# Retention attention and a Gelu MLP on one core: batches in pairs, units of 128 tokens, attention output made transposed in column tiles

## The chip, the core and the metric

The kernel runs on one core of one Trainium2 chip. The metric is device microseconds of that core for one execution; the median of several runs counts. TensorE (PE) multiplies matrices into PSUM; VectorE (DVE) and ScalarE (ACT) move and scale what lies in PSUM; GpSimd (POOL) issues the loads that convert float32 to bfloat16, and SyncE (SP) issues the other transfers.

## What is computed

A retention layer (attention without softmax, with a decay per head) and then a two-layer MLP with an exact Gelu:

```python
batch, n_heads, seq, head_dim = (8, 8, 576, 64)
scores = (1/sqrt(64)) * q @ k^T                       # per batch and head
gamma  = 1 - 2 ** (-5 - h)
D      = where(i >= j, gamma ** (i - j), 0)
x      = ((scores * D) @ v)  -> [8 * 576, 512]        # heads side by side
out    = gelu(x @ w_in) @ w_out                       # 512 -> 2048 -> 512, float32
```

The decay is separable: gamma^(i-j) = gamma^i * gamma^-j. So the sum over all earlier chunks of 128 tokens can be carried as a 64x64 state per head (sum of k^T v with v scaled), and within a chunk only a triangular mask is needed.

## The kernel before

Everything is written out by hand, in an order that a small planner at the end of the kernel chooses while the program is built; `manual_schedule` keeps that order on every engine. The planner holds one clock, `now`, for TensorE, with a fixed cost for each step, and times at which data should be ready (`at`, `x_at`, `land_chunk`, `land_in`, `land_out`).

Attention goes batch after batch in chunks of 128 tokens; a batch of 576 tokens has four full chunks and one of 64, so there are 40 chunks. For chunk i:
- `load_chunk`: three GpSimd loads (q, k, v); for chunk 0 three SyncE loads in float32.
- `turn` (step T): q and k transposed so that head_dim lies on partitions, on TensorE for the first 9 chunks (L213, copied out in L215 or L217), by a SyncE DMA transpose later (L207).
- `scores` and `masked` (step R, or RR for two chunks): eight matmuls with 64 rows of weights each (L226). Even and odd heads lie on partitions 0-63 and 64-127, so these are *row tiles*: two matmuls use one half of the array each. VectorE multiplies by the mask (L235), two products per chunk.
- `scaled_v` (step V): v times gamma^-j / 8 (L242).
- `inner` (step S): masked scores times v, eight matmuls of 64 columns (L260) with tokens on the output's partitions, and the state, four matmuls of 128 columns (L266) that compute two heads at once with two unused cross blocks; ScalarE copies the state out (L270).
- `cross`: q times the state of the chunks before, eight row-tiled matmuls of 64 columns (L280), added into the same PSUM banks.
- `evacuate`: VectorE scales by gamma^i (L288) into `x`, tokens on partitions. The MLP needs x transposed: `turn_x` on TensorE (step X, L302, copied in L303) for the first 9 chunks, a SyncE DMA transpose (L294) later.

The MLP goes over 9 blocks of 512 tokens. `mlp1_step`: four matmuls per 128 hidden units (L314), then Gelu on ScalarE (L318). `mlp2_step`: 16 matmuls per 128 tokens (L343), copied by ScalarE (L349) and stored by SyncE (L350); the last 128 tokens in three column pieces (L331 to L335). Blocks 0 and 1 are cut into pieces, so that they can start before all their tokens are there. In steady blocks the planner puts attention steps between MLP steps; a step RR stands in the second product of a block.

PSUM's eight banks are split: five (`a` to `e`) for transposes, scores, MLP; two for `o_ps`, one for `u_ps`. In the opening POOL builds an identity, two masks and three zeroed tiles before its first load, then loads chunks 1 to 3, the eight pieces of w_in, chunk 4, and w_out mixed with chunks 5 and 6. TensorE runs `warm` matmuls (L470) on zeros while it waits.

Of the kernel before, what the change touches and what calls it, by code (L numbers as in the profile page):

```python
# [13 lines left out]
ALU = mybir.AluOpType  # L14


@with_exitstack
def kernel(
# [13 lines left out]

# [8 lines left out]

# [4 lines left out]
    TOK_BLK = 512  # L46
    N_BLK = n_tok // TOK_BLK
    NCH = -(-S // C)
    chunks = [(b, ci, ci * C, min(C, S - ci * C)) for b in range(B) for ci in range(NCH)]
    N_CH = len(chunks)  # L50
    N_PE_TR = 9
    N_FIRST = 4
    N_LD = 7
    LEAD = 52
    PAIR_FROM = 2
    PAIR_LEAD = 70
    LATE_LEAD = 48
    log_gamma = [math.log(1.0 - 2.0 ** (-5.0 - h)) for h in range(H)]

    const_pool = ctx.enter_context(tc.tile_pool(name="const", bufs=1))  # L60
    ld_pool = ctx.enter_context(tc.tile_pool(name="ld", bufs=N_LD))
    tr_pool = ctx.enter_context(tc.tile_pool(name="tr", bufs=9))
    ret_pool = ctx.enter_context(tc.tile_pool(name="ret", bufs=2))
    v_pool = ctx.enter_context(tc.tile_pool(name="v", bufs=5))
    x_pool = ctx.enter_context(tc.tile_pool(name="x", bufs=4))
    u_pool = ctx.enter_context(tc.tile_pool(name="u", bufs=4))
    g_pool = ctx.enter_context(tc.tile_pool(name="g", bufs=2))
    o_pool = ctx.enter_context(tc.tile_pool(name="o", bufs=4))

    PS = bass.MemoryType.PSUM  # L70

    ps = ctx.enter_context(tc.tile_pool(name="ps", bufs=1, space=PS))

    xT = const_pool.tile([128, N_DM, n_tok], BF16, name="xT")


    zeros = const_pool.tile([128, 512], BF16, name="zeros")
    nc.vector.memset(zeros, 0.0)

    clock = [0.0]  # L80
    first = []
    for nm, src in (("q32", q), ("k32", k), ("v32", v)):
        t = const_pool.tile([128, H, D], FP32, name=nm)
        nc.sync.dma_start(t, src[0, :, 0:C, :].rearrange("h s d -> s h d"))
        first.append(t)
    ident = const_pool.tile([128, 128], BF16, name="ident")
    make_identity(nc, ident)

    lg_row = const_pool.tile([128, H, 1], FP32, name="lg_row")
    for h in range(H):  # L90
        nc.vector.memset(lg_row[:, h], log_gamma[h])
    ln_scale = const_pool.tile([128, 1], FP32, name="ln_scale")
    nc.vector.memset(ln_scale, math.log(scale))
    msk = const_pool.tile([128, 1, 128], FP32, name="msk")
    nc.vector.memset(msk, 1.0)

    pos = const_pool.tile([128, 1, NCH], FP32, name="pos")
    nc.gpsimd.iota(pos[:, 0, :], pattern=[[C, NCH]], base=0, channel_multiplier=1,
                   allow_small_or_imprecise_dtypes=True)

    nc.gpsimd.affine_select(
        out=msk[:, 0, :], in_=msk[:, 0, :], compare_op=ALU.is_ge, fill=0.0, base=0,
        pattern=[[1, 128]], channel_multiplier=-1,
    )

    arg = const_pool.tile([128, H, NCH], FP32, name="arg")
    nc.vector.tensor_tensor(arg, lg_row.to_broadcast([128, H, NCH]), pos.to_broadcast([128, H, NCH]), op=ALU.mult)
    dv = const_pool.tile([128, H, NCH], FP32, name="dv")
    nc.scalar.activation(dv, arg, AF.Exp, scale=-1.0, bias=ln_scale)
    dq = const_pool.tile([128, H, NCH], FP32, name="dq")  # L110
    nc.scalar.activation(dq, arg, AF.Exp)

    warm_act = const_pool.tile([128, 1], FP32, name="warm_act")
    nc.scalar.activation(warm_act, ln_scale, AF.Gelu)


    ret_short = [const_pool.tile([128, HP, 128], BF16, name=f"ret_short{e}") for e in range(2)]
    vh_short = const_pool.tile([128, H, D], BF16, name="vh_short")
    for t in ret_short + [vh_short]:
        nc.gpsimd.memset(t, 0.0)  # L120


    loaded = {}
    land_chunk, land_in, land_out = {}, [], []
    dma_clock = [2.0]

    def load_chunk(i, now=0.0):
        b, ci, c0, cs = chunks[i]
        qk = ld_pool.tile([128, 2, H, D], BF16, tag="qk", name="qk_ld")
        if i == 0:  # L130
            v_ld = first[2]
            nc.vector.tensor_copy(qk[:, 0], first[0])
            nc.vector.tensor_copy(qk[:, 1], first[1])
        else:
            v_ld = ld_pool.tile([128, H, D], BF16, tag="v", name="v_ld")
            for dst, src in ((qk[:, 0], q), (qk[:, 1], k), (v_ld, v)):
                nc.gpsimd.dma_start(dst[:cs], src[b, :, c0:c0 + cs, :].rearrange("h s d -> s h d"))  # L137
        loaded[i] = (qk, v_ld)
        dma_clock[0] = max(dma_clock[0], now) + 3.0 * cs / C
        v_at = 6.5 if i == 0 else dma_clock[0] + (1.2 if i < N_FIRST else 1.6)  # L140
        land_chunk[i] = (v_at - 1.9, v_at - 0.9, v_at)

    W_IN_COLS = 256
    w_in_sb, w_out_sb = [], []

    def load_w_in():
        j = len(w_in_sb)
        t = const_pool.tile([128, N_DM, W_IN_COLS], BF16, name=f"w_in{j}")
        nc.gpsimd.dma_start(
            t, moe_w_in[:, j * W_IN_COLS:(j + 1) * W_IN_COLS].rearrange("(c p) f -> p c f", p=128)  # L150
        )
        w_in_sb.append(t)
        dma_clock[0] += 1.38
        land_in.append(dma_clock[0] + (1.9 if j else 1.3))

    def load_w_out():
        j = len(w_out_sb)
        t = const_pool.tile([128, 2, d_model], BF16, name=f"w_out{j}")
        nc.gpsimd.dma_start(
            t, moe_w_out[j * 256:(j + 1) * 256, :].rearrange("(c p) f -> p c f", p=128)  # L160
        )
        w_out_sb.append(t)
        dma_clock[0] += 1.38
        land_out.append(dma_clock[0] + 1.3)

    for i in range(4):
        load_chunk(i)
    for _ in range(d_ff // W_IN_COLS):
        load_w_in()
    load_chunk(4)  # L170
    for j in range(N_DF // 2):
        load_w_out()
        if j in (3, 6):
            load_chunk(5 + (j == 6))
    


    st = {i: {} for i in range(N_CH)}
    u_ps = [None]
    mlp_begun = [False]  # L180

    free_at = dict.fromkeys("abcde", 0.0)
    held = set()
    last_tag = [None]

    def first_free(n=1):
        return sorted((x for x in free_at if x not in held), key=lambda x: free_at[x])[:n]

    def bank(until, shape, dtype, name):

        tag = last_tag[0] = first_free()[0]
        free_at[tag] = clock[0] + until
        return ps.tile(shape, dtype, tag=tag, name=name)

    def tr_ps(shape, name):

        return bank(1.3, shape, BF16, name)

    def turn(i, parts=(0, 1)):

        cs = chunks[i][3]
        qk = loaded[i][0]
        if "qkT" not in st[i]:
            st[i]["qkT"] = tr_pool.tile([128, 2, HP, 128], BF16, tag="qkT", name="qkT")
        qkT = st[i]["qkT"]
        if i >= N_PE_TR:
            nc.sync.dma_start(qkT.rearrange("p j hp s -> p (j hp) s")[:, :, :cs],  # L207
                              qk[:cs].rearrange("p j h d -> p (j h d)"), transpose=True)
            return
        for j in parts:  # L210
            ps = tr_ps([128, HP, 128], "qk_ps")
            for hp in range(HP):
                nc.tensor.transpose(ps[:, hp, :cs], qk[:cs, j, 2 * hp:2 * hp + 2, :], ident[:cs, :cs])  # L213
            if i >= N_FIRST:
                nc.vector.tensor_copy(qkT[:, j, :, :cs], ps[:, :, :cs])  # L215
            else:
                nc.scalar.copy(qkT[:, j, :, :cs], ps[:, :, :cs])  # L217

    def scores(i, banks):
        cs = chunks[i][3]  # L220
        qkT = st[i]["qkT"]
        sc = [ps.tile([128, HP, 128], FP32, tag=banks[e], name=f"sc{e}") for e in range(2)]
        for hp in range(HP):
            for e in range(2):
                sl = slice(64 * e, 64 * e + 64)
                nc.tensor.matmul(sc[e][:cs, hp, :cs], lhsT=qkT[sl, 1, hp, :cs], rhs=qkT[sl, 0, hp, :cs],  # L226
                                 start=True, stop=True)
        return sc

    def masked(i, sc):  # L230
        b, ci, c0, cs = chunks[i]
        st[i]["ret"] = []
        for e in range(2):
            r = ret_short[e] if cs < C else ret_pool.tile([128, HP, 128], BF16, tag=f"ret{e}", name=f"ret{e}")
            nc.vector.tensor_tensor(r[:cs, :, :cs], sc[e][:cs, :, :cs],  # L235
                                    msk[:cs, :, :cs].to_broadcast([cs, HP, cs]), op=ALU.mult)
            st[i]["ret"].append(r)

    def scaled_v(i):
        b, ci, c0, cs = chunks[i]  # L240
        vh = vh_short if cs < C else v_pool.tile([128, H, D], BF16, tag="vh", name="vh")
        nc.vector.tensor_tensor(vh[:cs], loaded[i][1][:cs],  # L242
                                dv[:cs, :, ci:ci + 1].to_broadcast([cs, H, D]), op=ALU.mult)
        st[i]["vh"] = vh

    def by_parity(i):

        lo = HP * st[i]["half"]
# [358 lines left out]
```

## Time and profile before

| what | value |
|---|---|
| median of the runs (311.76 to 313.3) | 312.15 us |
| span of the profiled execution | 444.2 us |
| mean granted TensorE clock in it | 0.658 |
| VectorE, ScalarE, GpSimd busy | 101.9, 143.3, 112.4 us |
| packets of GpSimd's loads (60% of 16 engines' span) | 17.97 MB |
| packets of SyncE's transfers (22.5%) | 21.05 MB |
| x transposes by DMA (L294): issues, us to landing | 31, 3.5 |
| q and k transposes by DMA (L207) | 31, 5.0 |
| output stores (L350), 256 KB each | 35, 2.4 |

Each run is timed without the profiler; the profile is one more execution, and this one took longer than the timed ones, at a lower clock. "PEclk" is the clock that TensorE was granted, in tenths of full speed. A line of the timeline gives start, duration, engine, source line, output<-input, and in brackets the idle time before it and what ended that. Matmuls are pipelined, so their durations overlap; the distance between starts is the pace.

### The profile page before, as it was taken

How to read it: one execution, taken by the hardware profiler on the slowest of the kernel's cores; microseconds unless marked ns; L12 is line 12 of the kernel's file. 1: busy time of each engine (PE TensorE's matmuls, PEld its weight loads, DVE VectorE, ACT ScalarE, POOL GpSimd, SP SyncE). 2: the span in 40 equal slices, each digit the busy share in tenths (PEclk: the TensorE clock that was granted, in tenths of full speed). 3: DMA queues.
4: the chain of work that ended last, by engine and by line, in shares of the span. 5: the costliest groups of instructions: out<-in, count | busy, mean ns of one | idle time of the engine just before them, and what ended most of it. 6: DMA issues, size and time to landing. Idle time of an engine off the chain costs nothing.

```text
span 444.2 us, 6130 instructions
## 1 busy us (share of the span) xinstructions
PE 436.6 (98%) x2522; PEld 204.9 (46%) x2522; DVE 101.9 (23%) x189; ACT 143.3 (32%) x279; POOL 112.4 (25%) x144
## 2 busy tenths in 40 slices
PE   7999999999999999999999999999999999999997
PEld 3676358855534444344433443344434333333334
DVE  4601345345332240034402500063102100000000
ACT  5664025523244213421343124311442134114411
POOL 9878524426242316004620440000000000000000
PEclk8666666666666666666666666666666666666666
DMA  9999979959999989519990991042101200010011
GB/s 136 179 189 178 127 107 144 90 62 158 159 154 72 110 105 155 60 35 167 127 161 1 121 176 47 0 84 72 41 0 49 66 25 0 24 47 26 0 46 49
DMA packets 168636, 39.40 MB, mean 89 GB/s; under 512 B 157600, under 2 KB 164128, under 8 KB 168608
## 3 DMA queue, kind: packets, MB, share of 16 engines
q0 software_dynamic: 115792, 17.97, 59.8%
q1 hardware_dynamic: 52816, 21.05, 22.5%
q8 instruction: 19, 0.31, 0.3%
q14 instruction: 9, 0.07, 0.1%
HBM read 36.70 MB, written 9.44 MB: 104 GB/s over the span
## 4 chain that ended last, share of the span: by engine, by line
PE 95%; DVE 2%; DMA 1%; POOL 1%; issue 1%; ACT 0%; DVEq 0%
PE hT L314 42%; PE oT L343 41%; PE o_ps L260 3%; PE u_ps L266 2%; PE o_ps L280 1%; PE oT L331 1%; DMA qk_ld<-in_k_dram 1%; PE qk_ps L213 1%; PE x_ps L302 0%; DVE x L288 0%; DVE vh L242 0%; DVE qkT L215 0%; POOL qk_ld L137 0%; DVE ret_966 L235 0%; DVE ret_425 L235 0%
## 5 line engine op out<-in xcount | busy, mean ns | idle before, releaser
L137 POOL DMA_DIRECT2D qk_ld<-in_q_dram x39 | 33.5, 859 | 143.7 <-PE u_ps L266 107.4
L349 ACT COPY o_sb<-oT 128x512 f32<-128x512 f32 x35 | 20.5, 585 | 138.4 <-PE oT L343 132.7
L137 POOL DMA_DIRECT2D v_ld<-in_v_dram x39 | 34.0, 872 | 1.4 <-DMA w_in_153<-in_moe_w_in_dram 0.7
L137 POOL DMA_DIRECT2D qk_ld<-in_k_dram x39 | 33.6, 861 | 0.9 <-DMA w_in_151<-in_moe_w_in_dram 0.5
L270 ACT CAST u_sb<-u_ps 128x512 bf16<-128x512 f32 x32 | 18.7, 585 | 43.9 <-PE u_ps L266 43.3
L288 DVE TENSOR_TENSOR x<-o_ps,dq 128x512 bf16<-128x512 f32 (+1 forms) x40 | 26.4, 681 | 24.5 <-PE o_ps L280 14.5
L314 PE MATMUL hT<-xT,w_in_149 128*128 128x512 bf16 (+3 forms) x96 | 25.8, 429 | 0.5 <-DMA w_in_149<-in_moe_w_in_dram 0.5
L314 PE MATMUL hT<-xT,w_in_151 128*128 128x512 bf16 (+3 forms) x96 | 26.2, 431 | 0.0
L314 PE MATMUL hT<-xT,w_in_157 128*128 128x512 bf16 (+3 forms) x96 | 26.2, 432 | 0.0
L314 PE MATMUL hT<-xT,w_in_163 128*128 128x512 bf16 (+3 forms) x96 | 26.0, 432 | 0.0
L314 PE MATMUL hT<-xT,w_in_155 128*128 128x512 bf16 (+3 forms) x96 | 26.0, 428 | 0.0
L314 PE MATMUL hT<-xT,w_in_153 128*128 128x512 bf16 (+3 forms) x96 | 25.5, 423 | 0.3 <-DVE qkT L215 0.3
L314 PE MATMUL hT<-xT,w_in_159 128*128 128x512 bf16 (+3 forms) x96 | 25.5, 427 | 0.0
L314 PE MATMUL hT<-xT,w_in_161 128*128 128x512 bf16 (+3 forms) x96 | 25.5, 428 | 0.0
L242 DVE TENSOR_TENSOR vh<-v_ld,dv 128x512 bf16<-128x512 bf16 x31 | 20.8, 678 | 0.0
L314 PEld LDWEIGHTS <-w_in_159 128*128 128x128 bf16 x96 | 10.7, 117 | 13.4 <-issue 12.2
L314 PEld LDWEIGHTS <-w_in_163 128*128 128x128 bf16 x96 | 10.9, 121 | 12.8 <-issue 12.0
L314 PEld LDWEIGHTS <-w_in_157 128*128 128x128 bf16 x96 | 11.1, 122 | 12.5 <-issue 11.5
L314 PEld LDWEIGHTS <-w_in_149 128*128 128x128 bf16 x96 | 10.8, 119 | 12.9 <-issue 11.2
L314 PEld LDWEIGHTS <-w_in_161 128*128 128x128 bf16 x96 | 10.9, 120 | 12.4 <-issue 10.9
L314 PEld LDWEIGHTS <-w_in_155 128*128 128x128 bf16 x96 | 10.9, 121 | 12.2 <-issue 11.2
L314 PEld LDWEIGHTS <-w_in_151 128*128 128x128 bf16 x96 | 11.0, 120 | 11.5 <-issue 10.6
(814 smaller groups left out, 730.3 us busy)
## 6 DMA issues: line engine op xcount, KB each, us to landing
out_dram<-o_sb SPq DMA_DIRECT2D x35, 256.0 KB, 2.4
qk_ld<-in_q_dram POOLq DMA_DIRECT2D x31, 128.0 KB, 5.0
qk_ld<-in_k_dram POOLq DMA_DIRECT2D x31, 128.0 KB, 5.3
v_ld<-in_v_dram POOLq DMA_DIRECT2D x31, 128.0 KB, 5.5
qk_ld<-in_q_dram POOLq DMA_DIRECT2D x8, 64.0 KB, 5.5
qk_ld<-in_k_dram POOLq DMA_DIRECT2D x8, 64.0 KB, 6.2
v_ld<-in_v_dram POOLq DMA_DIRECT2D x8, 64.0 KB, 5.9
qkT<-qk_ld SPq DMA_TRANSPOSE x31, 5.0
```

Source lines behind the costliest of these rows:

```text
L137: nc.gpsimd.dma_start(dst[:cs], src[b, :, c0:c0 + cs, :].rearrange("h s d -> s h d"))
L213: nc.tensor.transpose(ps[:, hp, :cs], qk[:cs, j, 2 * hp:2 * hp + 2, :], ident[:cs, :cs])
L242: nc.vector.tensor_tensor(vh[:cs], loaded[i][1][:cs], dv[:cs, :, ci:ci + 1].to_broadcast([cs, H, D]), op=ALU.mult)
L260: nc.tensor.matmul(ov[:, e, hp, :], lhsT=s["ret"][e][:, hp, :], rhs=s["vh"][:, 2 * hp + e, :], start=(hp == 0 and mate is None), stop=(ci ...
L266: nc.tensor.matmul(u_ps[0][:, hp, :], lhsT=loaded[i][0][:cs, 1, 2 * hp:2 * hp + 2, :], rhs=s["vh"][:cs, 2 * hp:2 * hp + 2, :], start=(ci = ...
L270: nc.scalar.copy(u, u_ps[0])
L280: nc.tensor.matmul(ov[:cs, e, hp, :], lhsT=s["qkT"][sl, 0, hp, :cs], rhs=s["u"][sl, hp, 64 * e:64 * e + 64], start=False, stop=(hp == HP - 1),
L288: nc.vector.tensor_tensor(x.rearrange("p hp e d -> p e hp d")[:cs], by_parity(i)[:cs], dq.rearrange("p (hp e) c -> p e hp c", e=2)[:cs, :, ...
L314: nc.tensor.matmul(hT[:, :hi - lo], lhsT=w[:, cc, o:o + 128], rhs=xT[:, cc, tok0 + lo:tok0 + hi], start=(cc == 0), stop=(cc == N_DM - 1))
L331: nc.tensor.matmul(oT[:, :hi - lo], lhsT=g_tiles[t, m][:, ts * 128:(ts + 1) * 128], rhs=w_out_sb[m // 2][:, m % 2, lo:hi], start=(m == 0), ...
L343: nc.tensor.matmul(oT, lhsT=g_tiles[t, m][:, ts * 128:(ts + 1) * 128], rhs=w_out_sb[m // 2][:, m % 2, :], start=(m == 0), stop=(m == N_DF ...
L349: nc.scalar.copy(o_sb, oT)
```

## The change

Batches are taken in pairs. A *unit* has 128 tokens: (pair, chunk, one of the two batches), and the two 64-token ends of a pair make one unit together, with a mask that keeps the batches apart. That gives 36 units, all full, and 512 MLP tokens are always 4 units; xT's columns are in the order of units, and an output tile of a joined end is stored with two transfers.

The matmuls of attention change sides. In `inner`, v is the weight (64 columns) and the masked scores stream (128 columns), so the output has head_dim on partitions: even heads in partitions 0-63, odd ones in 64-127, which are *column tiles*. The state is made in column tiles too, only the blocks that are used, and ScalarE copies two halves into a block-diagonal tile whose other blocks were zeroed once. `cross` is then four matmuls on the whole array. The output is what the MLP takes, so `evacuate` writes xT directly, and the x transposes and `turn_x` are gone. The scale gamma^i now runs along columns (`dqT`).

```diff
+    for bp in range(B // 2):
+        for ci in range(NCI - 1):
+            groups.append([len(units), len(units) + 1])
+            units += [(bp, ci, 0), (bp, ci, 1)]
+        groups.append([len(units)])
+        units.append((bp, NCI - 1, None))
...
-                nc.tensor.matmul(ov[:, e, hp, :], lhsT=s["ret"][e][:, hp, :], rhs=s["vh"][:, 2 * hp + e, :],
-                                 start=(hp == 0 and mate is None), stop=(ci == 0 and hp == HP - 1), skip_group_check=True)
+                nc.tensor.matmul(o[64 * e:64 * e + 64, hp, :], lhsT=vals[:, 2 * hp + e, :], rhs=s["ret"][e][:, hp, :],
+                                 start=(hp == 0), stop=(ci == 0 and hp == HP - 1), skip_group_check=True)
...
-                nc.tensor.matmul(u_ps[0][:, hp, :], lhsT=loaded[i][0][:cs, 1, 2 * hp:2 * hp + 2, :],
-                                 rhs=s["vh"][:cs, 2 * hp:2 * hp + 2, :], start=(ci == 0 and hp == 0),
+                nc.tensor.matmul(u_ps[64 * e:64 * e + 64, j, hp, :], lhsT=loaded[i][0][:, 1, 2 * hp + e, :],
+                                 rhs=s["vh"][:, 2 * hp + e, :], start=(ci == 0 and j == 0 and hp == 0),
...
-            nc.scalar.copy(u, u_ps[0])
+        u = u_sb[ci % 2]
+        for e in range(2):
+            sl = slice(64 * e, 64 * e + 64)
+            nc.scalar.copy(u[sl, j, :, 64 * e:64 * e + 64], u_ps[sl, j])
...
-                nc.tensor.matmul(ov[:cs, e, hp, :], lhsT=s["qkT"][sl, 0, hp, :cs],
-                                 rhs=s["u"][sl, hp, 64 * e:64 * e + 64], start=False, stop=(hp == HP - 1),
+                nc.tensor.matmul(o[:, hp, cols], lhsT=u[:, jj, hp, :], rhs=s["qkT"][:, 0, hp, cols],
+                                 start=False, stop=(hp == HP - 1), skip_group_check=True)
...
-            nc.sync.dma_start(xT[:, :, col:col + cs], x[:cs].rearrange("p hp e d -> p (hp e d)"), transpose=True)
+            nc.vector.tensor_tensor(dst, o, by, op=ALU.mult)
```

In the numbers of the changed kernel, scores are L281, their masks L294, inner L317, the state L329 and its copies L337, cross L359, evacuation L369 and L377, MLP L393, L398 and L430. Two units (`N_RAW`) at the start take the decay in the mask (`near`) and use v unscaled, and ScalarE copies their output.

The opening: POOL has two iotas ahead of its first load. The identity, masks and exponents are derived from an iota by VectorE and ScalarE; the table `dqT` by four exponentials for its second chunk and by GpSimd products with a step factor for the others. v of the first unit is loaded by GpSimd.

```diff
-    for i in range(4):
-        load_chunk(i)
-    for _ in range(d_ff // W_IN_COLS):
-        load_w_in()
-    load_chunk(4)
-    for j in range(N_DF // 2):
-        load_w_out()
-        if j in (3, 6):
-            load_chunk(5 + (j == 6))
+    ORDER = ("q1 k1 v0 v1 q2 k2 q3 k3 wi0 v2 v3 wi1 wi2 wi3 wi4 wi5 wi6 wi7 dq2 q4 k4 v4 wo0 wo1 wo2 dq3 q5 k5 v5 wo3 wo4 "
+             "q6 k6 v6 wo5 wo6 dq4 dq0 q7 k7 v7 wo7 q8 k8 v8")
...
+    near = const.tile([128, 2, HP, 128], FP32, name="near")
+    nc.scalar.activation(near, arg, AF.Exp, bias=ln_scale)
...
+    for hp in range(HP):
+        nc.scalar.activation(dqT[:, hp, C:2 * C], val[:, 0, :], AF.Exp, scale=lgT[:, hp], bias=off[:, hp])
...
+            nc.gpsimd.tensor_tensor(dqT[:, :, i * C:i * C + n], dqT[:, :, o * C:o * C + n],
+                                    by.to_broadcast([128, HP, n]), op=ALU.mult)
```

The planner is new (the "emission model"): it keeps a clock for TensorE, ScalarE, VectorE and GpSimd each (`T`), adds a cost when TensorE goes between full, row-tiled and column-tiled matmuls (`pe`), and takes all eight PSUM banks as one stock with a time at which each is free (`free_at`, `held`). Its steps are A (scores, for one or two units, with inner, state and cross of the units before when they are ready), B (inner), U (state), X (cross and evacuation) and T (a half of a transpose):

```diff
+            elif kind == "A":
+                g, back = a
+                for i in back:
+                    inner(i)
+                    nB += 1
+                    if units[i][1] < NCI - 1:
+                        to_state.append(i)
+                for i in to_state[:]:
+                    to_state.remove(i)
+                    state(i)
+                for i in g:
+                    scores(i)
+                    nA += 1
+                for n, i in enumerate(g):
+                    masked(i)
+                    if n == 0:
+                        for x in back:
+                            cross(x)
+                            evacuate(x)
+                            nX += 1
```

The first 8 units are transposed on TensorE (`either` copies them out on VectorE or ScalarE, whichever is free first), the other 28 by DMA. MLP blocks 0 and 1 are cut into two halves of 256 tokens.

## The prediction

> **What bounds the kernel now.** I read the page's busy rows and clock row first, then the chain of waits, then the timeline of the opening and of one attention step.
>
> ```profile
> span 444.2 us, 6130 instructions
> ...
> PE 436.6 (98%) x2522; PEld 204.9 (46%) x2522; DVE 101.9 (23%) x189; ACT 143.3 (32%) x279; POOL 112.4 (25%) x144
> ...
> PE   7999999999999999999999999999999999999997
> ...
> PEclk8666666666666666666666666666666666666666
> ...
> PE 95%; DVE 2%; DMA 1%; POOL 1%; issue 1%; ACT 0%; DVEq 0%
> ```
>
> TensorE is busy 98% of the span and is 95% of the chain that ended last. But this execution had a granted clock of about 0.65 and took 444.2 us; the timed runs' median is 312.15. So I count TensorE's work in streamed columns and price them at both clocks. Two pieces of the chain give the slow price:
>
> ```profile
> 357.76 20.91 PE hT L314 x64
> 378.67 20.91 PE oT L343 x64
> ```
>
> 64 matmuls of 512 columns in 20.91 us: 1.567 columns per ns at a granted 0.653, so 2.40 at clock 1.00. A burst in the opening agrees:
>
> ```profile
> 12.18 0.28 PE L260 MATMUL o_ps<-vh,ret_288 128*128 128x64 bf16 x4
> ...
> 12.29 0.28 PE L260 MATMUL o_ps<-vh,ret_290 128*128 128x64 bf16 x4
> ...
> 12.40 0.52 PE L266 MATMUL u_ps<-vh,qk_ld 128*128 128x128 bf16 x4
> ```
>
> Eight 64-column matmuls start between 12.18 and 12.40: 27.5 ns each, 2.33 per ns. The reader is to see also that their eight 128-column weight loads hid behind them.
>
> Columns before. MLP: 1152 x 512 = 589,824. Attention: scores 32 x 512 + 8 x 256 = 18,432 (a pair of row tiles starts together in L226, so it counts once); inner 40 x 512 = 20,480; state 32 x 512 = 16,384; cross 32 x 256 = 8,192 (pairs again); q and k transposes 8 x 1024 + 512 = 8,704; x transposes 8 x 512 + 256 = 4,352. That is 76,544, in all 666,368: 425.2 us at 1.567, 277.7 us at 2.40. So the timed runs hold 312.15 - 277.7 = 34.5 us that is not streaming at full clock (or their mean clock lies between 277.7/312.15 = 0.89 and 1). Of it the trace explains 23.2 us:
> - opening: the first MLP matmul starts at 17.52, after some 10,750 columns of attention (4.5 us at 2.40): 13.0;
> - 33 visits to row tiles, two switches each. In the steady part matmuls follow each other every 0.29 or 0.36 us; the row tile after the one at 158.49 came 0.46 later, at 158.95, so a switch costs 0.11: 66 x 0.11 = 7.3;
> - tail: last matmul ends about 441.3, span 444.2: 2.9.
>
> 11.3 us stay open: a clock just under 1, or waits that a slow TensorE hides here (after 24 us the profile's windows show only 0.85 us of idle TensorE).
>
> ```profile
> 3.25 1.01 POOL qk_ld L137
> 4.26 4.11 DMA qk_ld<-in_k_dram
> ...
> 11.38 0.82 POOL L149 DMA_DIRECT2D w_in_149<-in_moe_w_in_dram  x1
> ...
> 17.52 1.40 PE L314 MATMUL hT<-xT,w_in_149 128*128 128x256 bf16 x8 [0.54 <-DMA w_in_149<-in_moe_w_in_dram]
> ```
>
> The opening hangs on POOL's DMA queue: its first load is issued at 3.2 behind masks and memsets, the first weights at 11.38, and the MLP starts when those land.
>
> **The change, step by step.**
>
> *Columns.* 36 full units replace 40 chunks (64-token ends are joined). Scores 36 x 512 = 18,432. Inner has 8 matmuls of 128 columns with 64-wide weights, whose outputs lie in partitions 0-63 and 64-127; if such column tiles overlap in pairs as the row tiles do, 36 x 512 = 18,432. State 32 x 256 = 8,192 on the same condition. Cross becomes 4 full matmuls of 128 columns (8 of 64 for a joined end) on a block-diagonal state: 28 x 512 = 14,336. Transposes 8 x 1024 = 8,192; x transposes none. Total 67,584: 8,960 fewer, -5.7 us at 1.567 and **-3.7 us** at 2.40. No row here shows a column tile. Bounds by the nearest rows: full overlap as in L226; none as in L260 adds 18,432 + 8,192 = 26,624 columns, +11.1 us. I take full overlap, because operands and sizes are nearest to the row tiles.
>
> The trace first: six loads of 64-wide weights in row tiles of a short chunk passed, with their matmuls, between the starts at 38.08 and 38.19, 18 ns a load.
>
> ```profile
> 38.08 0.21 PE L226 MATMUL sc_671<-qkT 64*64 64x64 bf16 x1
> ...
> 38.19 0.19 PE L226 MATMUL sc_671<-qkT 64*64 64x64 bf16 x1
> ```
>
> [...] No run here shows a load in a column tile.
>
> *Switches.* In the order of the built program TensorE changes between full, row-tiled and column-tiled matmuls 85 times instead of 66: 19 x 0.11 = **+2.1 us**. Ends: 0 if column tiles switch free, +9.4 if every column switch costs twice (85 x 0.11 more).
>
> *Opening.* POOL now has two iotas ahead of its first load. The short iota took 0.13 us, the mask's select 0.31, so loads begin near 1.3 instead of 3.2: 1.9 us earlier. The first weights stand behind 8 loads (0.9 us each) instead of 9: 2.8 us earlier. The second piece stands behind v2 and v3, so only 0.9 us earlier. Between these I take **-1.8 us** (ends -2.8 and 0). Zero, because ScalarE's constants grow: it was free at 4.07 us; now one exponential of 1024 columns (two of the 0.585 us copies of 512), four of 128 (0.27 each, the final copy's row) and three small ones (0.22) make it free about 7 us, and the query copies may queue behind them; VectorE takes them if it is free earlier. Four dqT products on POOL stand before the last w_out load (bounds 0.5 us each, the 512-column memset row, to 1.2); it landed at about 43.3, and block 0's second product needs it at about 43 at full clock: 0 to 2 us, covered by the opening's upper end.
>
> *Moved at no cost.* Evacuation writes xT itself: 31 x transposes (1.2 us of SP's queue each, landing in 3.5) go, with 9 TensorE turns and their copies. Nobody waited for L294, so the cover was the lead of attention over the MLP; DMA engines get emptier. VectorE's products stay about four per unit at a pitch of 0.60 us. State copies become 64 of 256 columns (0.38, the same-sized Gelu) for 32 of 0.585: +5.6 us on ScalarE, which idles 138 us before its output copies. If that cover went, the Gelu and with it TensorE's banks would be late.
>
> *Tail.* The last unit's rows go to two batches, so each last piece has two DMA issues of 0.33: **+0.3 us**.
>
> *Hidden waits.* The new loop counts VectorE, ScalarE and bank times, takes all 8 PSUM banks as one stock and drops the x turns, one of which was late in the profile (0.52 us at 48.2 behind a qkT copy). Of the open 11.3 us I take a third, **-3.8** (ends -11.3 and 0): the x turns and x DMAs are about a third of what a chunk hands between engines.
>
> Sum: -3.7 + 2.1 - 1.8 + 0.3 - 3.8 = -6.9, so 312.15 becomes **305.3 us**. Against the profiled execution, without hidden waits: 444.2 - 5.7 + 2.1 - 1.8 + 0.3 = 439.1 us at the same granted clock.
>
> **Rivals.**
> 1. *Column tiles run one after another.* For: no row shows a column tile. Against: the row tiles of scores and cross start together, weights and moving data of the same sizes. +11.1 gives 316.4 us, slower. It decides once more than 62% of the overlap is missing (6.9 of 11.1).
> 2. *The waits come back*: the opening is held by ScalarE's constants, and the steady part keeps its 11.3 us. Left are -3.7 + 2.1 + 0.3: 310.8 us, no change by the measure below. For: the opening's loads land where DMA packets are already dense (178 to 189 GB/s in the second to fourth slice). Against: the loads that start it are issued earlier.
> 3. *The pair step waits for VectorE.* Inner of two units now heads TensorE's queue with states, scores and the next MLP matmuls behind it; two mask products late (2 x 0.60) in each of some 13 pair steps is +15.6: 320.9. Against: an MLP step of four matmuls is 0.85 us at full clock, and several lie between two pair steps.
>
> **How the numbers follow.** Forecast 0.68; rival 2 0.14; rival 1 0.13; rival 3 0.05. A measurement of this kernel tells about 0.5% from no change (1.6 us). The forecast's own range is 299 (6.3 of the 7.5 us of open waits that the sum keeps gone too) to 310.5. Rivals 1 and 3 hold 0.18, so the range ends at 314 and holds rival 2. Faster 0.68, same 0.14, slower 0.18.
>
> **What would show it.** L317 and L329 starting in pairs within a few ns, a unit's inner in about 0.23 us: right; eight starts 50 to 80 ns apart: rival 1. The first MLP matmul near 15 us shows the opening; TensorE idle over 1 us after 24 us, released by VectorE, shows rival 3. I am wrong altogether if the granted clock of the timed runs moves with the mix of matmuls.

## The result and the profile after

The changed kernel took 324.19 us (median of 4 runs, 321.51 to 325.44) against 312.73 us for the kernel before, run beside it (4 runs): ratio 1.0358, 95% interval 1.0302 to 1.0414. It is slower by 3.6%. The forecast was 305.3 us and the range ended at 314, so the direction was wrong and the time is outside the range.

The profiled execution of the changed kernel had a granted clock of 1.00, span 321.8 us. The one of the kernel before that stood behind the prediction was at 0.66, so the kernel before was profiled once more (run e0, below) and came at 1.00 this time, span 310.6 us. From here on, these two are compared. First the changed kernel's page: span, busy rows, the slices, the clock, the chain's shares.

```profile
span 321.8 us, 5686 instructions
...
PE 298.3 (93%) x2322; PEld 159.7 (50%) x2356; DVE 99.1 (31%) x181; ACT 145.3 (45%) x296; POOL 115.6 (36%) x144
...
PE   8989999996899888998999979988999999999993
...
PEclk9999999999999999999999999999999999999999
...
PE 70%; DMA 15%; POOL 7%; issue 3%; ACT 2%; DVE 0%; ACTq 0%; POOLq 0%; DVEq 0%
```

The same rows of the kernel before at the same clock:

```profile
span 310.6 us, 6130 instructions
...
PE 300.4 (97%) x2522; PEld 165.1 (53%) x2522; DVE 101.9 (33%) x189; ACT 141.6 (46%) x279; POOL 112.3 (36%) x144
...
PE   7789999899999999999999999999999999999996
```

The span grew by 11.2 us, and TensorE's busy time did not (298.3 against 300.4 us): the time went into idle TensorE. The changed kernel's trace lacks the records of 34 of its 2356 matmuls (x2322 beside x2356 weight loads), so its busy time is a little more than 298.3; the traces of e0 to e3 below lack none. The slices say where. Before, nearly every slice after the eighth is a 9; after, 8s, a 7 and a 6 are strewn over the middle of the span. The view by stretches makes numbers of it (columns: stretch, its length, then busy time and instructions of PE, PEld, DVE, ACT and POOL, granted clock, DMA share, GB/s). The changed kernel:

```profile
24.00:100.00 76.00, 71.02 (x654) 44.72 (x661) 31.71 (x53) 35.69 (x86) 52.51 (x64) 1.00 1.87 168
100.00:240.00 140.00, 129.90 (x1086) 66.46 (x1101) 50.85 (x83) 60.49 (x119) 40.91 (x50) 1.00 1.19 114
```

The kernel before (e0):

```profile
24.00:100.00 76.00, 74.38 (x819) 50.05 (x817) 37.34 (x69) 36.64 (x96) 48.88 (x59) 1.00 2.03 168
100.00:240.00 140.00, 139.81 (x1126) 70.56 (x1124) 50.88 (x87) 62.48 (x107) 43.24 (x52) 1.00 1.40 137
```

TensorE's idle time is the length minus its busy time. Between 100 and 240 us it is 10.10 us after and 0.19 before; between 24 and 100 us 4.98 and 1.62. After 24 us some 1.6 us of the changed kernel's idle time are gaps of 0.05 us at missing matmuls, for which the view of waits names no one (15.4 us by stretches up to 305 us, 13.8 by waits). Two lines of that view over the whole span (columns: who waits, for whom, us in total, times, longest):

```profile
PE u_ps L329 <- ACT u_sb L337: 10.1, 12, 0.9
...
PE o_ps L317 <- DVE ret L294: 1.6, 2, 1.3
```

Twelve times TensorE's state matmul (L329) waits for ScalarE's copy of a state (L337): once for 0.2 us in the opening, once for 0.8 between 24 and 100 us, and ten times for 0.9 between 100 and 240, which makes 9.1 of the 10.10 us there. One of these ten in the timeline (start, us, engine, line, operation; in brackets the idle time just before it and what ended it):

```profile
143.49 0.64 PE L317 MATMUL o_ps<-ret,vh 128*64 128x128 bf16 x16
143.96 0.29 PE L329 MATMUL u_ps<-vh,qk_ld 128*64 128x64 bf16 x8
144.35 0.76 ACT L337 CAST u_sb<-u_ps 64x256 bf16<-64x256 f32 x2 [1.02 <-PE u_ps L329]
...
145.16 0.32 PE L329 MATMUL u_ps<-vh,qk_ld 128*64 128x64 bf16 x8 [0.91 <-ACT u_sb L337]
145.40 0.62 PE L281 MATMUL sc<-qkT 64*128 64x128 bf16 x16
145.56 0.76 ACT L337 CAST u_sb<-u_ps 64x256 bf16<-64x256 f32 x2 [0.46 <-PE u_ps L329]
...
146.63 2.54 PE L430 MATMUL oT<-w_out,g 128*128 128x512 bf16 x11
```

This is a pair step. Inner of both units (16 matmuls), then the state of the first unit (8), then ScalarE copies that state, two copies of 0.38 us, from 144.35 to about 145.11. Only then, at 145.16, does the second unit's state begin. Both units write into one PSUM tile, u_ps, each into its own region, and the program gives them in the order state, copies, state, copies; the second state waits until the first state's copies have been read out. In the timeline scores (145.40), cross (145.96) and the MLP matmuls (from 146.63) follow behind that wait.

### The profile page after: what moved, and what is told of

It is laid out like the page before. It is cut to its first block, busy times and chain, and to the rows that moved or that the text cites. A ratio compares the mean times of both kernels' runs of the same rounds, so it can differ in the third digit from the quotient of the medians.

```text
span 321.8 us, 5686 instructions
## 1 busy us (share of the span) xinstructions
PE 298.3 (93%) x2322; PEld 159.7 (50%) x2356; DVE 99.1 (31%) x181; ACT 145.3 (45%) x296; POOL 115.6 (36%) x144
## 4 chain that ended last, share of the span: by engine, by line
PE 70%; DMA 15%; POOL 7%; issue 3%; ACT 2%; DVE 0%; ACTq 0%; POOLq 0%; DVEq 0%
PE oT L430 31%; PE hT L393 30%; DMA v_ld<-in_v_dram 9%; POOL qk_ld L196 4%; DMA qk_ld<-in_q_dram 3%; DMA w_in<-in_moe_w_in_dram 3%; ACT u_sb L337 2%; PE o_ps L317 2%; PE sc L281 2%; PE o_ps L359 2%; POOL v_ld L196 2%; PE u_ps L329 2%; POOL w_in L172 1%; PE oT L417 1%; PE qk_ps L260 1%
## 5 line engine op out<-in xcount | busy, mean ns | idle before, releaser
L393 PE MATMUL hT<-xT,w_in 128*128 128x512 bf16 (+1 forms) x697 | 127.1, 340 | 1.7 <-DMA w_in<-in_moe_w_in_dram 0.8
L430 PE MATMUL oT<-w_out,g 128*128 128x512 bf16 x535 | 123.0, 379 | 1.6 <-issue 0.5
L398 ACT ACTIVATE g<-hT 128x512 bf16<-128x512 f32 (+1 forms) x176 | 91.4, 519 | 37.5 <-PE hT L393 34.7
L393 PEld LDWEIGHTS <-w_in 128*128 128x128 bf16 x704 | 68.4, 98 | 58.0 <-DMA w_in<-in_moe_w_in_dram 1.2
L430 PEld LDWEIGHTS <-g 128*128 128x128 bf16 x560 | 53.3, 98 | 59.8
L294 DVE TENSOR_TENSOR ret<-sc,msk 128x512 bf16<-128x512 f32 x68 | 43.6, 683 | 83.7 <-PE sc L281 83.4
L337 ACT CAST u_sb<-u_ps 64x256 bf16<-64x256 f32 x64 | 23.5, 367 | 31.7 <-PE u_ps L329 30.7
L377 DVE TENSOR_TENSOR xT<-o_ps,dqT 128x512 bf16<-128x512 f32 x34 | 22.3, 683 | 6.8 <-PE o_ps L359 6.4
L329 PE MATMUL u_ps<-vh,qk_ld 128*64 128x64 bf16 x256 | 9.6, 196 | 10.2 <-ACT u_sb L337 10.1
L317 PEld LDWEIGHTS <-vh 128*64 128x64 bf16 x272 | 8.3, 109 | 10.8 <-issue 7.3
L317 PE MATMUL o_ps<-ret,vh 128*64 128x128 bf16 x272 | 12.2, 223 | 1.6 <-DVE ret L294 1.6
L281 PE MATMUL sc<-qkT 64*128 64x128 bf16 x288 | 12.4, 218 | 1.2 <-DMA qkT<-qk_ld 1.0
L329 PEld LDWEIGHTS <-qk_ld 128*64 128x64 bf16 x256 | 7.4, 111 | 11.6 <-issue 11.1
L281 PEld LDWEIGHTS <-qkT 64*128 64x128 bf16 x288 | 8.1, 94 | 4.9 <-DVE qkT L248 1.5
L359 PE MATMUL o_ps<-qkT,u_sb 128*128 128x128 bf16 (+1 forms) x128 | 9.8, 214 | 0.0
```

The source lines that it names most:

```text
L281: nc.tensor.matmul(got[e][1][:, hp, :], lhsT=qkT[sl, 1, hp, :], rhs=qkT[sl, 0, hp, :], start=True, stop=True)
L294: nc.vector.tensor_tensor(r, t, by, op=ALU.mult)
L317: nc.tensor.matmul(o[64 * e:64 * e + 64, hp, :], lhsT=vals[:, 2 * hp + e, :], rhs=s["ret"][e][:, hp, :], start=(hp == 0), stop=(ci == 0 an ...
L329: nc.tensor.matmul(u_ps[64 * e:64 * e + 64, j, hp, :], lhsT=loaded[i][0][:, 1, 2 * hp + e, :], rhs=s["vh"][:, 2 * hp + e, :], start=(ci == ...
L337: nc.scalar.copy(u[sl, j, :, 64 * e:64 * e + 64], u_ps[sl, j])
L377: nc.vector.tensor_tensor(dst, o, by, op=ALU.mult)
```

## The experiments

**e0, the kernel before, profiled again.** No edit.

> The kernel before, unchanged, profiled once more, so that both kernels can be compared at the clock of the timed runs. If this profile has a granted clock near 1.00, its span is about 310 us. My theory of the missed 11.3 us (waits that a slow TensorE hides) expects TensorE idle for some 8 to 11 us after 24 us, at x turns, qkT copies and weight loads. The rival (the timed runs' clock is a little under 1) expects a mean granted clock of 0.95 to 0.97 and hardly any idle time after 24 us.

Measured: the profile ran at clock 1.00 with a span of 310.6 us in a run of 313.52 us. After 24 us TensorE is idle 1.62 + 0.19 = 1.8 us (rows above). There is next to no hidden waiting in the kernel before: the expected 8 to 11 us are not there, and neither is the rival's clock of 0.95 to 0.97.

**e1, copies after both states.** In the pair step the state matmuls of both units are given first, and ScalarE's copies of both after them. The amounts of work and of PSUM stay as they were. The function `state` is split for this; the cut shows the loop that calls its halves.

```diff
...
-                for i in to_state[:]:
-                    to_state.remove(i)
-                    state(i)
+                both = to_state[:]
+                for i in both:
+                    to_state.remove(i)
+                    state(i, copies=False)
+                for i in both:
+                    state_copies(i)
```

> In the pair step the state matmuls of both units are emitted first and ScalarE's four copies after them; nothing else changes. Theory (the second unit's state waits because the first unit's copies read the same PSUM tile): the waits of L329 for L337 go from 10.1 us to under 1, and the time falls by 10 to 13 us, to 311 to 314. Rival (ScalarE's copies are simply slow or late, and the next user of the state waits instead): the idle time moves to cross or to the next scores, and the time falls by less than 3 us, to over 321.

Measured: 314.29 us (10 runs), ratio to before 1.0028 (0.9996 to 1.0061), 9.9 us less than the changed kernel (10.3 by the two ratios, of 312.7 us), at the lower end of the 10 to 13 that were expected. ScalarE, for which TensorE's states had waited 10.1 us, is no longer among those that they wait for; 0.2 us for VectorE's scaled v is left. The runs of e1 had lower granted clocks (0.981 to 0.997) than those of the changed kernel (0.994 to 1.000), so the clock does not make the gain. A pair step of e1 in the timeline:

```profile
147.59 0.64 PE L317 MATMUL o_ps<-ret,vh 128*64 128x128 bf16 x16
148.06 0.42 PE L329 MATMUL u_ps<-vh,qk_ld 128*64 128x64 bf16 x16
...
148.41 0.62 PE L281 MATMUL sc<-qkT 64*128 64x128 bf16 x16
```

And its stretch from 100 to 240 us:

```profile
100.00:240.00 140.00, 140.00 (x1154) 70.51 (x1153) 50.88 (x83) 67.31 (x129) 41.18 (x50) 1.00 1.22 115
```

The two states are now one group of 16 matmuls; scores start 0.82 us after inner instead of 1.91 (145.40 - 143.49), and TensorE has no idle time left in this stretch. So the step is 1.09 us shorter, of which the view had shown 0.91 as idle. Eleven steps of the changed kernel take 1.86 to 1.92 us from inner to scores, and all eleven take 0.82 in e1: 12.0 us by the starts. Most of this is found in the time, so the wait did not move elsewhere; one scores step that waits 3.2 us for a transpose in e1, 1.0 in the changed kernel, takes back a part. ScalarE does the same copies as before the edit (busy 145.6 us, 145.3 in the changed kernel): it was never their amount, only their place between two states.

**e2, last piece stored in one.** The last block takes its row tiles in the order 0, 1, 3, 2 and the special last tile is the third, so that the last rows are no joined end and leave with one store per piece.

```diff
-        if (t, ts) == (N_BLK - 1, 3):
+        if (t, ts) == (N_BLK - 1, 2):
...
-            runs.append([("2", t, ts, m, m + 4) for ts in range(4) for m in range(0, N_DF, 4)])
+            order = (0, 1, 3, 2) if t == N_BLK - 1 else range(4)
+            runs.append([("2", t, ts, m, m + 4) for ts in order for m in range(0, N_DF, 4)])
...
```

> In the last block the third 128 tokens are done last instead of the joined end, so that the three last pieces have one store each. Theory (six stores in a row on SP's queue at about 0.57 us each, instead of three of 0.33, make the tail): the time from the last copy's start to the end goes from 4.9 to 2.8 us and the time falls by 2 us, to 322. Rival (the store's landing makes the tail): under 0.5 us.

**e3, both edits.**

> Both edits. They lie at different places, so they should add: 12 to 15 us less than the changed kernel, 309 to 312 us, which is as fast as the kernel before or up to 1% faster. If the first edit only moves the wait, 319 to 321.

Measured: e2 alone 323.2 us (4 runs), 1.0326 (1.0277 to 1.0376), an interval that overlaps with the changed kernel's, so the gain of 1.0 us is not clear of the noise; 2 were expected. e3 311.93 us (10 runs), 0.9967 (0.9935 to 0.9999), 2.4 us less than e1. The end of the changed kernel, store queue and last output copy:

```profile
315.52 3.67 SPq L424 DMA_DIRECT2D out_dram<-o_sb  x6
...
316.91 0.27 ACT L421 COPY o_sb<-oT 128x128 f32<-128x128 f32 x1 [0.63 <-PE oT L417]
```

The end of e3:

```profile
304.17 2.01 SPq L431 DMA_DIRECT2D out_dram<-o_sb  x3
...
305.56 0.27 ACT L428 COPY o_sb<-oT 128x128 f32<-128x128 f32 x1 [0.63 <-PE oT L424]
```

From the start of the last copy to the end of the span it is 321.8 - 316.91 = 4.9 us in the changed kernel and 308.3 - 305.56 = 2.7 in e3 (in e0 310.6 - 307.78 = 2.8, in e2 321.8 - 319.06 = 2.7). The six stores of 64 rows hold SP's queue for 3.67 us, the three of 128 rows for 2.01, and they are issued one behind the other. So the joined end costs 2.1 us in the trace, and 1.0 to 2.4 in the times.

**e5, the opening's first load made late.** On top of e3, four memsets on GpSimd stand ahead of its first load.

```diff
+    late = const.tile([128, 512], BF16, name="late")
+    for _ in range(4):
+        nc.gpsimd.memset(late, 0.0)
```

> On top of both edits four memsets of 128x512 on GpSimd ahead of its first load, about 1.9 us, which puts the first load where the kernel before had it. Theory of the prediction (the earlier opening is worth 1.8 us): the time rises by 1.5 to 2 us. Rival (what the opening gains is lost again at the loads, which come at the DMA engines' pace): under 0.7 us.

Measured: 313.93 us (10 runs), 1.0033 (1.0011 to 1.0056), against 0.9967 and 0.9949 for the same kernel without the memsets (e3, and e9 below): 2.0 to 2.6 us more. Its opening in the timeline:

```profile
3.33 1.04 POOL L199 DMA_DIRECT2D qk_ld<-in_q_dram  x1
...
17.79 1.05 PE L403 MATMUL hT<-xT,w_in 128*128 128x256 bf16 x8
```

The first load was at 1.37 us in the changed kernel, and its first MLP matmul at 14.43:

```profile
1.37 1.04 POOL L196 DMA_DIRECT2D qk_ld<-in_q_dram  x1 [0.20 <-issue]
...
14.43 1.03 PE L393 MATMUL hT<-xT,w_in 128*128 128x256 bf16 x8
...
17.30 0.61 PE L393 MATMUL hT<-xT,w_in 128*128 128x256 bf16 x4 [0.76 <-DMA w_in<-in_moe_w_in_dram]
```

In e3 these two are at 1.38 and 15.01. A first load 1.95 us later moves the first MLP matmul by 2.8 us and costs 2.0 to 2.6 us at the end. A part of that is clock: the runs of e5 had granted clocks around 0.989, those of e3 and e9 around 0.994. At 1.00 it is 311.99 against 310.06 to 310.56 us (three runs of e3 and e9), at 0.994 it is 313.97 and 314.09 against a median of 311.53 (nine runs): 1.4 to 2.6 us. The opening hangs on GpSimd's queue, and most of a gain there is kept.

**e4, e7, e8: the late transposes.** In e3, TensorE's idle time between 24 and 100 us is 4.38 us. The timeline of e3 names most of it:

```profile
58.29 20.90 SPq L269 DMA_TRANSPOSE qkT<-qk_ld  x5
...
86.74 0.40 PE L281 MATMUL sc<-qkT 64*128 64x128 bf16 x8 [2.82 <-DMA qkT<-qk_ld]
...
91.07 13.97 PE L400 MATMUL hT<-xT,w_in 128*128 128x512 bf16 x64 [1.01 <-DVE xT L384]
```

Scores wait 2.82 us for a transpose of q and k. Five transposes hold SP's queue for 20.90 us, 4.2 us each. The planner that sets the order of the program takes q and k as ready 8.0 us after it has given their transpose by DMA. e4 (on e3) tells it 17.0; e7 (on e3) lets TensorE transpose 12 units instead of 8; e8 does both.

```diff
-        s["T", 0] = s["T", 1] = T["pe"] + 8.0
+        s["T", 0] = s["T", 1] = T["pe"] + 17.0
```

```diff
-    N_PE_TR = 8
+    N_PE_TR = 12
```

> On top of both edits the planner counts 17 us instead of 8 from the issue of a q and k transpose by DMA to its use. Only the order of the work changes. Theory (what is left of the loss is a scores step put on TensorE's queue 2.8 us before its transpose lands, with cross, evacuation and the next MLP block behind it): TensorE's idle time after 24 us falls from 4.4 us to under 2, and the time by 2 to 3 us, to 309 to 310. Rival (the loads themselves come too late, whatever the order): the wait moves to the start of an MLP block, and the time stays within 1 us of 311.9.

> On top of both edits units 8 to 11 are transposed on TensorE too instead of by DMA. Costs four times 0.45 us of TensorE, 1.8 us. If the late transposes are late because the DMA engines are full between 50 and 90 us, the waits of 3.8 us go and the time falls by 1 to 2 us, to 310 to 311; if loads alone set the pace, the time rises by 1 to 2 us, to 313 to 314.

> The order with 17 us for transposes by DMA, and units 8 to 11 transposed on TensorE. If both remedies act on the same wait, they do not add: the four turns cost up to 1.8 us and the time is 310 to 312 us. If some lateness is left that only fewer DMA transposes cure, 308 to 309.5 us.

e4 310.09 us (7 runs), 0.9928 (0.9906 to 0.9949); e7 311.33 us (10), 0.9961 (0.9943 to 0.998); e8 310.61 us (4), 0.9932 (0.9916 to 0.9948). The time of e4 is about as expected, that of e7 lies between its two expectations, and the two remedies of e8 do not add. As e3 had been timed beside other runs than e4, e3 and e4 were run once more on one chip:

> The two edits (state copies after both states, full tile last) once more, beside the others of this job, to set the earlier 311.93 us against the kernel with the later planner time. Expected 311 to 312.5 us, 1.5 to 2 us above the kernel that counts 17 us for its transposes.

> The kernel that counts 17 us, once more on the same chip as the run before it: 309.5 to 310.5 us. If the two kernels of this job lie within 0.7 us of each other, the planner's time is not what made the difference.

e9 (the kernel of e3) took 311.28 us (7), 0.9949 (0.9912 to 0.9986); e10 (that of e4) 310.99 us (4), 0.9938 (0.9916 to 0.996). They stand 0.3 us apart, so the planner's time is not shown to matter. What first set e3 and e4 1.8 us apart goes with the granted clock of the single runs: all seven runs of e4 were at 1.00 (309.08 to 311.01 us), and of the 17 of e3 and e9 the three at 1.00 took 310.06 to 310.56, the others, at 0.989 to 0.995, 311.11 to 313.57. Nor is the planner's effect on the wait shown: the stretch from 24 to 100 us holds 2.66 us of idle time in e4 (first fence), but 4.44 in e10, the same kernel (second fence).

```profile
24.00:100.00 76.00, 73.34 (x671) 46.11 (x670) 33.03 (x53) 36.75 (x88) 51.97 (x63) 1.00 1.88 166
```

```profile
24.00:100.00 76.00, 71.56 (x661) 45.09 (x659) 32.88 (x53) 35.29 (x85) 52.63 (x64) 1.00 1.90 169
```

That transposes are late is seen; what makes them late, and what would cure it, stays open. All of e3, e4, e7, e8, e9 and e10 lie below the kernel before, the versions with the planner's 17.0 us by 0.6 to 0.7%.

A PSUM tile of its own for the second unit's state, the other way to take the wait away, was not tried: the program gives every such tile a bank, and by its count the pair step would hold nine of eight (four for scores, two for `o_ps`, two for states, one for the MLP sum that is open).

## Why the prediction was wrong, by its own steps

**The step that failed: "Moved at no cost".** It costed the 64 state copies at nothing because ScalarE has idle time, and named as the risk a late Gelu. That was the wrong question. ScalarE had the time, but the copies of the first unit stand between two pieces of TensorE's work on one PSUM tile, and TensorE waits for the duration of two copies in each of the eleven pair steps that have two states: 9.9 us of idle time, 12.0 by the starts, and no term of the sum. Rival 3 had the place (the pair step heads TensorE's queue, with scores and MLP matmuls behind it) and the pattern (two operations late in each of some 13 steps), but took VectorE for the engine and 15.6 us for the price; it was given 0.05. Inner's waits for VectorE are 1.6 us in two places, and an MLP step waits 0.6 for it once: more than the 1 us that was to show rival 3, far less than its price, so that sign was too loose. The order of instructions of the built program showed state, copies, state, copies; what was missing was to ask, for every tile that two units share, who reads it between the two writes.

**"Hidden waits" (-3.8) was wrong too.** There was no reserve: at clock 1.00 TensorE idles 1.8 us in the kernel before. What the open 11.3 us are, as far as e0 tells: its chain has

```profile
252.41 13.81 PE hT L314 x64
```

which is 215.8 ns for 512 columns, 2.373 per ns and not the 2.40 that was scaled up from clock 0.65. All columns then take 666,368 / 2.373 = 280.8 us instead of 277.7 (+3.1). Run and span differ, which the prediction didn't count: by 2.9 us in e0's run (313.52 and 310.6), by 1.85 in the median of the 19 runs of the kernel before that were taken beside e1 to e3. With 1.85, and the 1.8 us of idle time, that is 6.8; 4.5 us stay unsettled.

**"Tail" (+0.3) was mis-sized**: 2.1 us in the trace. The issue of a 128-row store (0.33 us) was taken for that of a 64-row one, and one more issue was counted, not three; the last six take 0.47 to 0.59 us each, in series.

**"Opening" (-1.8) was right.** The first MLP matmul came at 14.43 us against 16.74 in e0, 2.3 earlier; the second weight piece then cost 0.76 us of it. e5 gives back 1.4 to 2.6 at like clocks.

**"Columns" and "Switches" (-3.7 + 2.1) were about right, as far as the runs tell.** No run has them alone. Column tiles overlap in pairs: in the changed kernel's pair step 16 inner matmuls of 128 columns pass in 143.96 - 143.49 = 0.47 us, 0.235 per unit where about 0.23 was forecast, so rival 1 is refuted. Their 64-wide weight loads hid: in the same trace 16 of them pass in 0.48 us from 143.49 on, beside the matmuls. e1 has the same weight loads and takes 9.9 us of the lost time back, so they are not what made the changed kernel slow.

The account closes within 1 us. Against e0 (span +11.2 us) the changed kernel has +12.0 us in eleven pair steps, other waits after 24 us of 3.4 us against 1.8 (+1.6), and +2.1 from the last copy on: 15.7. So opening, columns and switches gave 15.7 - 11.2 = 4.5 us; they were forecast at 3.4. e3 agrees: span -2.3, idle time +2.8 from 24 to 100 and -0.2 from 100 to 240, the end equal: 4.9 us given. The plan of the change was sound by 4 to 5 us; the waits and a longer end took more than three times that.

**Rival 2** ("The waits come back", 310.8) comes near the time of e3 (311.93 and 311.28), and this is luck: there the opening's gain was kept, and a late transpose of 2.8 us, not the 11.3 us of waits that it had in mind, took it back.

**The clock.** The prediction called itself wrong altogether if the granted clock of the timed runs moved with the mix of matmuls. It did not: 0.994 to 1.000 in the four runs of the changed kernel, and the same in the 19 of the kernel before. Only among the experiments does it differ more (0.981 to 0.997 in e1), and e1 is far faster than the changed kernel.

## What to carry to other kernels

Where two units come to share an accumulator tile, write down the order of its writes and reads on each engine: here a read of 0.76 us by an idle engine between two writes cost the writing engine 1.09 us each time, and giving both writes first cost nothing. Where two kernels' times differ as little as those of e3 and e4 (1.8 us of 312, which went with clocks of 0.989 to 0.995 against 1.00), compare runs of the same granted clock before naming a cause. Before counting on open time as a reserve, take it from a profile at the clock of the timed runs, and subtract what lies outside the span (1.85 us here). A store cut into two halves of the rows took 0.47 to 0.59 us of issue for each half, against 0.33 for the whole, and at the end of this kernel nothing hid it (2.1 us).

## What was not expected of the hardware

The kernel before was profiled once at a granted clock of 0.66 (444.2 us) and once at 1.00 (310.6 us), while all its timed runs lie within 311 to 316 us, at 0.994 to 1.00 where the clock was listed: here a profile came from a clock that the timed runs didn't have.

A write into one region of a PSUM tile waited for reads of another region, 0.8 to 0.9 us in each of 11 pair steps. Whether the chip needs that wait, or only the program's bookkeeping by tiles, these runs don't tell.

At the end of the kernel, store issues on SP took 0.47 to 0.59 us for 64 rows and 0.33 for 128. Earlier in the changed kernel the 128-row ones took 0.33 to 0.77.
